# Leaky ReLU in place in PSUM, its remainder on VectorE; one-input query maxima; ScalarE rounds the query exponentials

## The chip, the cores and the metric

The kernel runs on one core of one Trainium2 chip. The metric is the device time of one execution in microseconds (us); lower is better. The engines of the core are TensorE (PE in the profile; its weight loads have a row of their own, PEld), VectorE (DVE), ScalarE (ACT), GpSimd (POOL) and SyncE (SP, which issues the transfers). Each engine works through its own instructions in a fixed order. TensorE, VectorE and ScalarE reach PSUM, where products are accumulated; the operations of GpSimd in this kernel read and write SBUF alone.

## The reference

Two stages follow each other. The first is a linear attention with a feature map; the second is a two-layer network with a leaky ReLU between its products.

```python
def phi(x):                                   # batch 8, heads 8, 576 tokens, 64 wide
    proj = np.einsum('bhsd,df->bhsf', x, w_phi)           # 128 features
    proj = proj - np.max(np.abs(proj), axis=-1, keepdims=True)
    return np.concatenate([np.exp(proj), np.exp(-proj)], axis=-1)
q_p, k_p = (phi(q), phi(k))
kv = np.einsum('bhsf,bhsd->bhfd', k_p, v)
z = np.sum(k_p, axis=2)
num = np.einsum('bhsf,bhfd->bhsd', q_p, kv)
den = np.einsum('bhsf,bhf->bhs', q_p, z)[..., None] + 1e-06
attn = num / den                              # -> x: 4608 tokens x 512
h = x @ w_in                                  # 512 -> 2048
g = np.maximum(0.01 * h, h)
out = g @ w_out                               # 2048 -> 512
```

## The kernel before, in words

**Products in pieces.** Most operands of TensorE are given as a rounded part and a remainder: a value `x` becomes `xh` (a cast to the matmul type fp32r) and `xl = x - xh`, and a product is the sum of `xh*wh`, `xh*wl` and `xl*wh`. The helper `copy_` makes the casts and `tt_` the remainders; all their instructions carry the helper's lines, L67 (ScalarE), L69 (VectorE) and L72 (subtractions and other two-input operations, VectorE or GpSimd), so they are told apart by the names of their tiles. The table `ENG` says which engine takes which key, in turn where several letters stand (`a` ScalarE, `v` VectorE, `p` GpSimd); a copy without an entry goes to ScalarE, a subtraction without one to GpSimd.

**The network.** The 4608 tokens are 18 blocks of 256, and the 2048 hidden features 16 pieces of 128; one step is one piece of one block, 288 steps in all. `layer1` makes 12 products of 256 columns into a PSUM bank `h` (two banks in turn), four each on L615, L616 and L618. ScalarE's Prelu on L622 writes the leaky ReLU to `g` in SBUF, ScalarE casts `gh` from it, and GpSimd takes `gl = g - gh`. `g`, `gh` and `gl` have two buffers each. `layer2` makes 6 products of 512 columns from `gh` and `gl` (L635, L636, L637) into the two `acc` banks of the block, and is called three steps (`LAG`) behind `layer1`. At the end of a block the two banks are copied to `o` and sent out.

**The attention.** It goes by pairs of heads, 32 in all. The first eight pairs have their own forms (`first_k_phase`, `first_q_phase`, `token_q_phase`); the other 24 go through `q_phase`. There the projections of the queries are transposed in blocks of 32x32 by VectorE (L380), a maximum of absolute values is taken in each block row (L382), and six small operations (L384 to L389) bring the maxima of the four groups of 32 partitions together: three copies and two two-input maxima from and to other partitions, then the result is copied back to all 128. L396 subtracts it, L398 transposes back, and ScalarE makes the two exponentials `eq` (L403, L404). `qh` is the cast of `eq`, on VectorE by the table's entry; `ql = eq - qh` is on GpSimd; L415 to L418 multiply them with the sums of the keys. L424 to L427 make the reciprocal, and the quotient goes to the `ring`, from which `split` takes `xh` and `xl` for the network. `k_phase` does the same for keys (L202 to L295) and is advanced together with the queries of the pair before.

**Order.** The kernel is recorded step by step, and a planner then sets the order of each engine's instructions by priorities and its own estimate of durations: attention has a higher priority than the network, so its instructions go first wherever the planner holds them to be ready. The order is fixed when the program is built; on the chip an instruction that waits holds up all that stand behind it on its engine.

Of the kernel before, what the change touches and what calls it, by code (L numbers as in the profile page):

```python
# [9 lines left out]
F32 = mybir.dt.float32  # L10
# [3 lines left out]
AF = mybir.ActivationFunctionType  # L14
ALU = mybir.AluOpType
AX = mybir.AxisListType

P = 128
# [7 lines left out]
T = 256  # L26
# [5 lines left out]
NK = 8  # L32
BUFS = {"kph": 2, "eq": 2, "m4": 2, "g": 2, "gh": 2, "gl": 2, "ql": 2}
PBUFS = {"a": 3, "c": 1, "h": 2, "acc": 2}
ENG = {"vh": "a", "kst": "v", "qh": "v", "o": "av", "kl": "pv", "kpl": "pppv", "ksub": "vvp", "l": "v"}
TINY = 2.0 ** -15
HUGE = 2.0 ** 16 * 1.875
PF = -10 ** 6
# [6 lines left out]
def attention_moe_kernel(ctx: ExitStack, tc: tile.TileContext, q, k, v, vt, w_phi, w_in, w_out, out):  # L45
    nc = tc.nc
# [4 lines left out]
    def ct(shape, dt, name):  # L51
        return cp.tile(shape, dt, tag=name, name=name)

    def st(shape, dt, tag):
        return sp.tile(shape, dt, tag=tag, name=tag, bufs=BUFS.get(tag, 1))
# [3 lines left out]
    def pick(key):  # L59
        n = cnt[key] = cnt.get(key, -1) + 1  # L60
        e = ENG.get(key, "")
        return e[n % len(e)] if e else None

    def copy_(key, o, i):
        e = pick(key) or "a"
        if e == "a":
            nc.scalar.copy(o, i)  # L67
        else:
            (nc.vector if e == "v" else nc.gpsimd).tensor_copy(o, i)  # L69

    def tt_(key, o, a, b, op):
        (nc.vector if pick(key) == "v" else nc.gpsimd).tensor_tensor(o, a, b, op=op)  # L72

    def pt(tag):
        return ps.tile([P, 512], F32, tag=tag, name=tag, bufs=PBUFS[tag])
# [5 lines left out]
    def weight(which, part, ft):  # L81
        g, f = divmod(ft, 4)
        if (which, part, g) not in weights:
            name = f"w{which}{part}{g}"
            weights[which, part, g] = (cp.tile([P, 4, DM], F32R, tag="late", name=name, bufs=4) if g == 3 else
                                       ct([P, 4, DM], F32R, name))
        return weights[which, part, g][:, f]
# [8 lines left out]
    vh = ct([P, 10, 66], F32R, "vh")  # L96
# [44 lines left out]
    for j in range(2):  # L141
        r = slice(64 * j, 64 * j + 64)
        c = slice(F * j, F * j + F)
# [39 lines left out]
    def load_q(i):  # L183
        rq = st([P, S], F32, "rq")
        nc.sync.dma_start(rq, q[i])
        qraw[i] = rq
# [112 lines left out]
    def blocks(x):  # L299
        return x.rearrange("p a b -> p (a b)").rearrange("p (c d) -> p c d", d=32)  # L300
# [60 lines left out]
    def q_phase(i):  # L361
        b, hp = divmod(i, NP)
        rq = qraw.pop(i)
        qs = st([P, 2, S], F32R, "qs")
        for j in range(2):
            o, n = slice(64 * j, 64 * j + 64), slice(64 - 64 * j, 128 - 64 * j)
            copy_("qx", qs[o, j], rq[o])
            nc.vector.tensor_tensor(qs[n, j], rq[o], qs[o, j].bitcast(F32), op=ALU.subtract)  # L368
        if i + 1 < B * NP:
            load_q(i + 1)  # L370
        yield
        tq = st([P, 2, 2, U], F32, "tq")
        m = st([P, 2, 18], F32, "m")
        for j in range(2):
            for u in range(2):
                pq = pt("a")[:, 0:U]
                rs = qs[:, j, U * u : U * u + U]
                nc.tensor.matmul(pq, lhsT=wq_h, rhs=rs, start=True, stop=False)
                nc.tensor.matmul(pq, lhsT=wq_l, rhs=rs, start=False, stop=True)
                nc.vector.transpose(tq[:, j, u], pq)  # L380
                yield
            nc.vector.tensor_reduce(m[:, j], blocks(tq[:, j]), axis=AX.X, op=ALU.max, apply_absolute_value=True)  # L382
        ms = st([64, 2, 18], F32, "ms")
        nc.vector.tensor_copy(ms, m[64:128])  # L384
        nc.vector.tensor_tensor(m[0:64], m[0:64], ms, op=ALU.max)
        nc.vector.tensor_copy(ms[0:32], m[32:64])
        nc.vector.tensor_tensor(m[0:32], m[0:32], ms[0:32], op=ALU.max)
        nc.vector.tensor_copy(m[32:64], m[0:32])
        nc.vector.tensor_copy(m[64:128], m[0:64])  # L389
        yield  # L390
        kvh, kvl = kvs_of[i]
        dn = tq[:, 0]
        qhs = st([P, 2, 2, U], F32R, "qh")
        for j in range(2):
            tj = blocks(tq[:, j])
            nc.vector.tensor_tensor(tj, tj, m[:, j].unsqueeze(2).broadcast_to([P, 18, 32]), op=ALU.subtract)  # L396
            mb = st([P, 2, U], F32, "mb")
            nc.vector.transpose(mb.rearrange("p a b -> p (a b)"), tq[:, j].rearrange("p a b -> p (a b)"))  # L398
            yield
            es = []  # L400
            for u in range(2):
                eq = st([P, 2, U], F32, "eq")
                nc.scalar.activation(eq[:, 0], mb[:, u], AF.Exp)  # L403
                nc.scalar.activation(eq[:, 1], mb[:, u], AF.Exp, scale=-1.0)  # L404
                qh = qhs[:, u]
                ql = st([P, 2, U], F32R, "ql")
                copy_("qh", qh, eq)
                tt_("ql", ql, eq, qh.bitcast(F32), ALU.subtract)
                es.append((qh, ql))
                yield  # L410
            for u in range(2):
                qh, ql = es[u]
                nm = pt("a")[:, 0:U]
                for t in range(2):
                    nc.tensor.matmul(nm, lhsT=kvh[:, j, t], rhs=qh[:, t], start=t == 0, stop=False)  # L415
                    nc.tensor.matmul(nm, lhsT=kvl[:, j, t], rhs=qh[:, t], start=False, stop=False)
                for t in range(2):
                    nc.tensor.matmul(nm, lhsT=kvh[:, j, t], rhs=ql[:, t], start=False, stop=t == 1)  # L418
                rr = slice(64 * j, 64 * j + 64)
                nc.scalar.copy(ring[rr, b % 2, hp, U * u : U * u + U], nm[0:64])  # L420
                nc.scalar.activation(dn[rr, u], nm[64:128], AF.Copy, bias=1e-6)
                yield
        dt = st([P, 2, U], F32, "mb")
        nc.vector.transpose(dt.rearrange("p a b -> p (a b)"), dn.rearrange("p a b -> p (a b)"))  # L424
        rc = st([P, 18], F32, "rc")
        nc.vector.reciprocal(rc, blocks(dt)[:, :, 0])
        nc.vector.transpose(blocks(dt), rc.unsqueeze(2).broadcast_to([P, 18, 32]))  # L427
        x = ring[:, b % 2, hp]
        tt_("x", x, x, dt.rearrange("p a b -> p (a b)"), ALU.mult)
        yield  # L430
# [153 lines left out]
    def attention():  # L584
        for i in range(NP, B * NP + 1):
            gens = [k_phase(i)] if i < B * NP else []
            if i > NP:
                gens.append((token_q_phase if i - 1 < NN else q_phase)(i - 1))
            while gens:
                for it in list(gens):  # L590
                    if next(it, end) is end:
                        gens.remove(it)
                    else:
                        yield i - 1
            yield i
# [16 lines left out]
    def layer1(i, ft):  # L612
        ph = pt("h")[:, 0:T]
        for d in range(NP):
            nc.tensor.matmul(ph, lhsT=weight(0, "h", ft)[:, d * P : d * P + P], rhs=xh[:, d], start=d == 0, stop=False)  # L615
            nc.tensor.matmul(ph, lhsT=weight(0, "l", ft)[:, d * P : d * P + P], rhs=xh[:, d], start=False, stop=False)  # L616
        for d in range(NP):
            nc.tensor.matmul(ph, lhsT=weight(0, "h", ft)[:, d * P : d * P + P], rhs=xl[:, d], start=False, stop=d == NP - 1)  # L618
        g = st([P, T], F32, "g")
        gh = st([P, T], F32R, "gh")  # L620
        gl = st([P, T], F32R, "gl")
        nc.scalar.activation(g, ph, AF.Prelu, alpha=0.01)  # L622
        copy_("gh", gh, g)
        tt_("gl", gl, g, gh.bitcast(F32), ALU.subtract)
        gs[i, ft] = (gh, gl)

    def layer2(i, ft, half=range(TT)):
# [47 lines left out]
    for n, (i, ft) in enumerate(steps):  # L675
        layer1(i, ft)
        advance(min(room(i + 1), NP * (1 + (i + (ft + 1) / NFT) * T / S) + 2))
        if ft == NFT - 1 and i + 1 < NBLK:
            advance(math.ceil((i + 2) * T / S) * NP)
            split(i + 1)  # L680
        if n >= LAG:
            layer2(*steps[n - LAG])
# [39 lines left out]
```

## Time and profile before

| | us |
|---|---|
| median of 3 runs (lowest, highest) | 1253.36 (1252.39, 1255.06) |
| profiled execution | 1253.03 |
| span of its instructions | 1251.2 |
| PE busy | 1184.7 (95%) |
| DVE busy | 840.5 (67%) |
| ACT busy | 804.3 (64%) |
| POOL busy | 691.0 (55%) |

The profile shows one execution. The shares are means over parts that differ: up to about 300 us the first pairs and the conversion of the weights run, from 300 to about 1060 us attention and network are interleaved, and from about 1080 us on only the network is left. A row of the groups reads: line, engine, operation, written tile, read tiles, shapes, count, then busy time in us and the mean of one in ns, then the idle time before these instructions and what ended it. A matmul's row has its whole length, though the next starts earlier, so short stalls of TensorE do not show as idle time in it.

### The profile page before, as it was taken

Reading aid. Unit: us, or ns where it says so; the run is one execution under the profiler, and the core shown is the slowest. Engines: PE = TensorE matmul, PEld = TensorE weight load, DVE = VectorE, ACT = ScalarE, POOL = GpSimd, SP = SyncE. Lnnn points to the kernel's source line nnn. Section 1 sums busy time; section 2 is a strip of 40 time slices with the busy share of each in tenths; the row PEclk is TensorE's granted clock in tenths of the full one; section 3 lists DMA queues with packets and bytes.
Section 4 is the critical chain, followed back from the end, with each engine's and each line's share of the span. In section 5 each row is a group of like instructions: output and inputs, shape, how many; then the busy total and the mean of one; then the engine's idle time right before and its main releaser. Section 6 shows DMA issues by size and latency. Waiting matters only on the chain. (4 is left out here: it accounts for less than half of the span.)

```text
span 1251.2 us, 21516 instructions
## 1 busy us (share of the span) xinstructions
PE 1184.7 (95%) x7654; PEld 1045.7 (84%) x7654; DVE 840.5 (67%) x1349; ACT 804.3 (64%) x2048; POOL 691.0 (55%) x724
## 2 busy tenths in 40 slices
PE   6889899999998999899999999999999999999998
PEld 5577688898887888788898888899997889999997
DVE  7999843478788877788888788854888887300000
ACT  6897865767667776666776667764776767433232
POOL 3233232457685776666676677764676867433232
PEclk9999999999998999999999999999999999999999
DMA  6544510211111101111111111020111110000000
GB/s 189 155 125 140 141 52 13 57 31 30 47 31 47 29 29 31 30 39 29 48 30 48 31 39 39 10 58 28 30 24 37 28 38 1 18 17 1 18 17 18
DMA packets 62779, 57.02 MB, mean 46 GB/s; under 512 B 45136, under 2 KB 46288, under 8 KB 62672
## 3 DMA queue, kind: packets, MB, share of 16 engines
q1 hardware_dynamic: 62672, 55.65, 15.8%
q8 instruction: 60, 0.98, 0.3%
q14 instruction: 47, 0.39, 0.1%
HBM read 46.20 MB, written 9.44 MB: 44 GB/s over the span
## 5 line engine op out<-in xcount | busy, mean ns | idle before, releaser
L72 POOL TENSOR_TENSOR gl<-g,gh 128x256 fp32r<-128x256 f32 x288 | 242.4, 846 | 275.1 <-ACT gh L67 214.7
L615 PE MATMUL h<-xh,w0h 128*128 128x256 f32 x1152 | 295.2, 284 | 6.7 <-ACT dn L567 2.2
L616 PE MATMUL h<-xh,w0l 128*128 128x256 f32 x1152 | 293.5, 282 | 1.3 <-DVE w0l L72 1.3
L615 PEld LDWEIGHTS h<-xh,w0h 128*128 128x128 f32 x1152 | 217.9, 189 | 18.7 <-ACT dn L567 3.0
L635 PE MATMUL acc<-w1h,gh 128*128 128x512 f32 x576 | 229.5, 399 | 2.9 <-DVE o L69 1.8
L636 PE MATMUL acc<-w1l,gh 128*128 128x512 f32 x576 | 228.0, 396 | 0.0
L616 PEld LDWEIGHTS h<-xh,w0l 128*128 128x128 f32 x1152 | 218.0, 189 | 11.5 <-DVE w0l L72 2.1
L637 PE MATMUL acc<-w1h,gl 128*128 128x512 f32 x576 | 218.3, 396 | 0.2 <-POOL gl L72 0.2
L618 PE MATMUL h<-xl,w0h 128*128 128x256 f32 x1152 | 201.7, 283 | 0.7 <-POOL xl L72 0.7
L622 ACT ACTIVATE g<-h 128x256 f32<-128x256 f32 x288 | 108.1, 383 | 133.0 <-PE h L618 93.1
L72 POOL TENSOR_TENSOR ql<-eq,qh 128x576 fp32r<-128x576 f32 x96 | 153.0, 1601 | 71.8 <-DVE qh L69 59.8
L618 PEld LDWEIGHTS h<-xl,w0h 128*128 128x128 f32 x1152 | 164.7, 189 | 3.1 <-POOL xl L72 2.0
L67 ACT CAST gh<-g 128x256 fp32r<-128x256 f32 x288 | 114.8, 404 | 70.4 <-PE acc L636 68.5
L72 POOL TENSOR_TENSOR kpl<-ek,kph 128x512 fp32r<-128x512 f32 x72 | 104.3, 1449 | 34.6 <-ACT kph L67 17.3
L635 PEld LDWEIGHTS acc<-w1h,gh 128*128 128x128 f32 x576 | 108.8, 189 | 16.7 <-DVE o L69 2.7
L637 PEld LDWEIGHTS acc<-w1h,gl 128*128 128x128 f32 x576 | 105.7, 188 | 19.1 <-POOL gl L72 1.3
L636 PEld LDWEIGHTS acc<-w1l,gh 128*128 128x128 f32 x576 | 109.1, 189 | 12.8
L69 DVE CAST qh<-eq 128x576 fp32r<-128x576 f32 x96 | 95.6, 1002 | 35.7 <-ACT eq L404 24.7
L250 ACT ACTIVATE ek<-pmk 128x256 f32<-128x256 f32 (+1 forms) x128 | 53.4, 417 | 64.8 <-POOL kpl L72 27.5
L69 DVE COPY o<-acc 128x512 f32<-128x512 f32 x17 | 11.5, 677 | 124.2 <-DMA out_dram<-o 124.0
L403 ACT ACTIVATE eq<-mb 128x288 f32<-128x288 f32 x96 | 42.2, 439 | 81.6 <-DVE mb L398 77.9
L72 POOL TENSOR_TENSOR ring<-ring,mb 128x576 f32<-128x576 f32 (+2 forms) x45 | 52.1, 1158 | 66.7 <-DVE mb L573 18.3
(227 smaller groups left out, 2505.6 us busy)
## 6 DMA issues: line engine op xcount, KB each, us to landing
out_dram<-o SPq DMA_DIRECT2D x35, 256.0 KB, 2.0
rk<-in_k_dram SPq DMA_DIRECT2D x30, 288.0 KB, 2.8
ring<-in_w_in_dram SPq DMA_DIRECT2D x16, 512.0 KB, 3.6
qh<-in_w_out_dram SPq DMA_DIRECT2D x16, 512.0 KB, 3.6
rq<-in_q_dram SPq DMA_DIRECT2D x28, 288.0 KB, 2.9
rv<-in_v_dram SPq DMA_DIRECT2D x30, 256.0 KB, 3.5
rv<-in_vt_dram SPq DMA_DIRECT2D x60, 32.0 KB, 2.9
f<-in_k_dram SPq DMA_DIRECT2D x2, 288.0 KB, 4.2
```

Source lines behind the costliest of these rows:

```text
L67: nc.scalar.copy(o, i)
L69: (nc.vector if e == "v" else nc.gpsimd).tensor_copy(o, i)
L72: (nc.vector if pick(key) == "v" else nc.gpsimd).tensor_tensor(o, a, b, op=op)
L250: nc.scalar.activation(ek[r, :, 0:F], pmk[r, 2 * s : 2 * s + 2], AF.Exp)
L403: nc.scalar.activation(eq[:, 0], mb[:, u], AF.Exp)
L615: nc.tensor.matmul(ph, lhsT=weight(0, "h", ft)[:, d * P : d * P + P], rhs=xh[:, d], start=d == 0, stop=False)
L616: nc.tensor.matmul(ph, lhsT=weight(0, "l", ft)[:, d * P : d * P + P], rhs=xh[:, d], start=False, stop=False)
L618: nc.tensor.matmul(ph, lhsT=weight(0, "h", ft)[:, d * P : d * P + P], rhs=xl[:, d], start=False, stop=d == NP - 1)
L622: nc.scalar.activation(g, ph, AF.Prelu, alpha=0.01)
L635: nc.tensor.matmul(a, lhsT=gh[:, ts], rhs=weight(1, "h", ft), start=ft == 0, stop=False)
L636: nc.tensor.matmul(a, lhsT=gh[:, ts], rhs=weight(1, "l", ft), start=False, stop=False)
L637: nc.tensor.matmul(a, lhsT=gl[:, ts], rhs=weight(1, "h", ft), start=False, stop=ft == NFT - 1)
```

## The change

The leaky ReLU is written back to its own PSUM bank `h`. ScalarE casts `gh` from there, and the remainder `gl = h - gh` is an operation of VectorE on the bank and `gh`; the tile `g` is gone. The query maxima are brought together by reductions: a copy is a maximum over one element, and a maximum of two is a reduction over two values that lie side by side in one tile, for which `m` and `ms` get a second half. The table gives `qh` to ScalarE.

```diff
-ENG = {"vh": "a", "kst": "v", "qh": "v", "o": "av", "kl": "pv", "kpl": "pppv", "ksub": "vvp", "l": "v"}
+ENG = {"vh": "a", "kst": "v", "qh": "a", "o": "av", "kl": "pv", "kpl": "pppv", "ksub": "vvp", "l": "v"}
 ...
-        m = st([P, 2, 18], F32, "m")
+        mm = st([P, 2, 2, 18], F32, "m")
+        m = mm[:, 0]
 ...
-        ms = st([64, 2, 18], F32, "ms")
-        nc.vector.tensor_copy(ms, m[64:128])
-        nc.vector.tensor_tensor(m[0:64], m[0:64], ms, op=ALU.max)
-        nc.vector.tensor_copy(ms[0:32], m[32:64])
-        nc.vector.tensor_tensor(m[0:32], m[0:32], ms[0:32], op=ALU.max)
-        nc.vector.tensor_copy(m[32:64], m[0:32])
-        nc.vector.tensor_copy(m[64:128], m[0:64])
+        def one(o, x):
+            nc.vector.tensor_reduce(o, x.unsqueeze(3), axis=AX.X, op=ALU.max)
+
+        ms = st([64, 2, 2, 18], F32, "ms")
+        one(mm[0:64, 1], m[64:128])
+        nc.vector.tensor_reduce(ms[0:64, 0], mm[0:64].rearrange("p s j c -> p j c s"), axis=AX.X, op=ALU.max)
+        one(ms[0:32, 1], ms[32:64, 0])
+        nc.vector.tensor_reduce(m[0:32], ms[0:32].rearrange("p s j c -> p j c s"), axis=AX.X, op=ALU.max)
+        one(m[32:64], m[0:32])
+        one(m[64:128], m[0:64])
 ...
-        g = st([P, T], F32, "g")
         gh = st([P, T], F32R, "gh")
         gl = st([P, T], F32R, "gl")
-        nc.scalar.activation(g, ph, AF.Prelu, alpha=0.01)
-        copy_("gh", gh, g)
-        tt_("gl", gl, g, gh.bitcast(F32), ALU.subtract)
+        nc.scalar.activation(ph, ph, AF.Prelu, alpha=0.01)
+        copy_("gh", gh, ph)
+        nc.vector.tensor_tensor(gl, ph, gh.bitcast(F32), op=ALU.subtract)
```

The planner orders all engines anew. In the changed kernel the lines stand up to five further down (L618 becomes L622, L637 becomes L640, the Prelu is L625, and `gl` is L627). Two places are spoken of below. The first is VectorE in `q_phase`, in the interleaved part, from the maxima to the next transposition (`tq` the transposed projections, `m` and `ms` the maxima, `mb` what the exponentials read; `kvl` and `qs` belong to other work). Before:

```order
L385 TENSOR_TENSOR m<-m,ms 64x36
L368 TENSOR_TENSOR qs<-rq,qs 64x576
L386 COPY ms<-m 32x36
L387 TENSOR_TENSOR m<-m,ms 32x36
L388 COPY m<-m 32x36
L294 TENSOR_TENSOR kvl<-c,kvh 128x4x64
L295 TENSOR_TENSOR kvl<-c,kvh 128x4x64
L389 COPY m<-m 64x36
L396 TENSOR_TENSOR tq<-tq,m 128x576 x2
L398 STREAM_TRANSPOSE mb<-tq 128x576
L69 CAST qh<-eq 128x576 x2
L398 STREAM_TRANSPOSE mb<-tq 128x576
```

And of the change:

```order
L385 TENSOR_REDUCE m<-m 64x36
L294 TENSOR_TENSOR kvl<-c,kvh 128x4x64
L295 TENSOR_TENSOR kvl<-c,kvh 128x4x64
L389 TENSOR_REDUCE ms<-m 64x36
L385 TENSOR_REDUCE ms<-ms 32x36
L627 TENSOR_TENSOR gl<-h,gh 128x256
L391 TENSOR_REDUCE m<-ms 32x36
L385 TENSOR_REDUCE m<-m 32x36
L385 TENSOR_REDUCE m<-m 64x36
L400 TENSOR_TENSOR tq<-tq,m 128x576 x2
L402 STREAM_TRANSPOSE mb<-tq 128x576
L627 TENSOR_TENSOR gl<-h,gh 128x256
```

The two casts `qh` between the transpositions are gone, and remainders `gl` now stand among the steps of the query, where VectorE had none.

The second place is TensorE at the start of block 16 (step 256), near the end, where only the network is left. Before, `h_14122` and `h_14147` are the first two steps of the block, and products of the old block (`gh_14078`, `gh_14103` and their remainders) follow:

```order
L618 MATMUL h_14122<-xl_71,w0h0_716 128x256
L618 MATMUL h_14147<-xl_71,w0h0_716 128x256 x2
L635 MATMUL acc_13806<-w1h3_1005,gh_14078 128x512
L636 MATMUL acc_13806<-w1l3_1006,gh_14078 128x512
L637 MATMUL acc_13806<-w1h3_1005,gl_14079 128x512
L635 MATMUL acc_13807<-w1h3_1005,gh_14078 128x512
L636 MATMUL acc_13807<-w1l3_1006,gh_14078 128x512
L637 MATMUL acc_13807<-w1h3_1005,gl_14079 128x512
L635 MATMUL acc_13806<-w1h3_1005,gh_14103 128x512
L636 MATMUL acc_13806<-w1l3_1006,gh_14103 128x512
```

In the change the same steps are `h_13866` and `h_13890`, and `gh_13879` is the cast of `h_13866`:

```order
L640 MATMUL acc_13562<-w1h3_1005,gl_13848 128x512
L622 MATMUL h_13866<-xl_71,w0h0_716 128x256
L622 MATMUL h_13890<-xl_71,w0h0_716 128x256
L640 MATMUL acc_13563<-w1h3_1005,gl_13848 128x512
L638 MATMUL acc_13962<-w1h0_729,gh_13879 128x512
L639 MATMUL acc_13962<-w1l0_730,gh_13879 128x512
L619 MATMUL h_13914<-xh_70,w0h0_716 128x256
L620 MATMUL h_13914<-xh_70,w0l0_717 128x256
```

ScalarE's rows for these two steps in the change:

```order
L625 ACTIVATE h_13866<-h_13866 128x256
L625 ACTIVATE h_13890<-h_13890 128x256
L67 CAST gh_13879<-h_13866 128x256
L67 CAST gh_13903<-h_13890 128x256
```

Before, all the products of two older steps stand between the first two steps of the block and the third; in the change a product that needs the cast `gh_13879` stands two rows behind the last product of `h_13866`, and the third step `h_13914`, which takes the bank of `h_13866`, two rows further.

## Prediction

> **What bounds the kernel now.** I read the busy time by stretches first. Columns: stretch, its length, then busy us of each engine.
>
> ```profile
> core 0: us, PE busy (x) PEld busy (x) DVE busy (x) ACT busy (x) POOL busy (x), PEclk, DMA share, GB/s
> 0.00:300.00 300.00, 272.62 (x1668) 229.01 (x1669) 220.16 (x400) 217.61 (x516) 108.31 (x136) 0.98 0.34 96
> 300.00:1060.00 760.00, 725.23 (x4803) 648.13 (x4802) 604.48 (x921) 522.97 (x1366) 517.13 (x501) 1.00 0.12 33
> 1100.00:1200.00 100.00, 100.00 (x637) 90.42 (x636) 1.38 (x2) 32.83 (x89) 34.80 (x53) 1.00 0.03 11
> ```
>
> At the end (1100 to 1200 us) TensorE never stops, VectorE is free, and nothing but fewer products would help. From 300 to 1060 us TensorE idles 760 - 725.23 = 34.8 us, with VectorE busy 80% of the time, ScalarE 69%, GpSimd 68%. A matmul's row is longer than its turn, which the chain of waits shows: in the last part four products of 256 columns take 0.48 us, 0.12 each, and one of 512 columns 0.24, while the row of L615 further down has a mean of 284 ns for 256 columns. So the idle time of PE leaves out most of a short stall.
>
> ```profile
> 1102.77 0.48 PE h L618 x4
> 1103.24 0.24 PE acc L635
> 1105.59 0.48 PE h L618 x4
> ```
>
> (These also give a step without attention: 1105.59 - 1102.77 = 2.82 us.) The weight loads are shorter than their turn, so their waits show more. The list of waits of PEld from 300 to 1060 us has 27 rows, sum 63.4 us (engine, tile and line that waited, what ended it, us in total, times, longest); the first ten and the last:
>
> ```profile
> PEld c L212 <- issue: 6.7, 9, 2.0
> PEld c L212 <- POOL kpl L72: 5.6, 8, 2.1
> PEld a L378 <- DVE tq L380: 5.2, 6, 1.3
> PEld a L415 <- ACT tq L421: 5.1, 7, 1.3
> PEld a L415 <- DVE pmk L237: 4.9, 9, 0.8
> PEld a L415 <- DVE qh L69: 4.8, 9, 0.9
> PEld a L418 <- POOL ql L72: 4.7, 9, 1.0
> PEld c L212 <- ACT kph L67: 4.0, 9, 1.1
> PEld acc L635 <- DVE o L69: 2.7, 3, 1.5
> PEld a L232 <- ACT tq L421: 2.5, 5, 0.8
> ...
> PEld a L232 <- issue: 0.2, 1, 0.2
> ```
>
> Summed by releaser: VectorE 23.0, GpSimd 13.6, ScalarE 17.9, the rest 8.9. TensorE is the bound, and loses about 63 us in this part to attention results that come later than its fixed order has them, mostly from VectorE and GpSimd.
>
> **Why these two are late.** Durations of VectorE's operations from the views by tile (count, then minimum/median/maximum ns):
>
> ```profile
> L69 DVE CAST qh<-eq x96: 441/990/1700, 275.1 to 1073.2; 128x576 fp32r<-128x576 f32 x96
> L202 DVE TENSOR_TENSOR ks<-rk,ks x48: 752/1717/1967, 213.4 to 1019.5; 64x576 fp32r<-64x576 f32 x48
> L386 DVE COPY ms<-m x24: 170/328/1312, 269.3 to 1063.3; 32x36 f32<-32x36 f32 x24
> L382 DVE TENSOR_REDUCE m<-tq x48: 705/753/755, 261.7 to 1062.0; 128x18 f32<-128x576 f32 x48
> ```
>
> Copies and two-input operations between SBUF tiles are stretched by up to 1.0 to 1.3 us for the same work, about one GpSimd operation (its groups below take 0.85 to 1.6 us); the reduction never is (705 to 755). So while GpSimd works, some forms of VectorE stand still.
>
> **The change, part by part.** The groups that carry its prices (mean ns after the busy time):
>
> ```profile
> L72 POOL TENSOR_TENSOR gl<-g,gh 128x256 fp32r<-128x256 f32 x288 | 242.4, 846 | 275.1 <-ACT gh L67 214.7 <-issue 16.0 <-PE acc L637 11.9
> L72 POOL TENSOR_TENSOR ql<-eq,qh 128x576 fp32r<-128x576 f32 x96 | 153.0, 1601 | 71.8 <-DVE qh L69 59.8 <-PE acc L636 9.9 <-PE a L418 1.3
> L615 PE MATMUL h<-xh,w0h 128*128 128x256 f32 x1152 | 295.2, 284 | 6.7 <-ACT dn L567 2.2 <-ACT w0h L67 2.0 <-ACT xh L67 1.7
> L67 ACT CAST gh<-g 128x256 fp32r<-128x256 f32 x288 | 114.8, 404 | 70.4 <-PE acc L636 68.5
> L622 ACT ACTIVATE g<-h 128x256 f32<-128x256 f32 x288 | 108.1, 383 | 133.0 <-PE h L618 93.1 <-POOL gl L72 36.2 <-PE a L232 1.5
> L69 DVE CAST qh<-eq 128x576 fp32r<-128x576 f32 x96 | 95.6, 1002 | 35.7 <-ACT eq L404 24.7 <-POOL ql L72 4.4 <-POOL gl L72 3.8
> L237 DVE TENSOR_TENSOR pmk<-a,pmk 128x256 f32<-128x256 f32 x96 | 37.1, 406 | 7.5 <-ACT pmk L67 6.5
> L240 DVE TENSOR_REDUCE m<-pmk 128x4 f32<-128x512 f32 x48 | 32.7, 681 | 1.3
> L240 DVE TENSOR_REDUCE m<-pmk 64x2 f32<-64x256 f32 x24 | 10.0, 417 | 0.8
> L67 ACT CAST qs<-rq 64x576 fp32r<-64x576 f32 x48 | 32.3, 673 | 4.1 <-PE a L379 3.4
> L67 ACT COPY pmk<-a 128x256 f32<-128x256 f32 x96 | 32.6, 373 | 3.4 <-PE a L232 2.8
> ```
>
> And how much of it lies between 300 and 1060 us (`gl` with its PE, PEld and POOL columns; `qh` with DVE's; the four maxima steps L384 to L387 with DVE's):
>
> ```profile
> 300.00:1060.00 760.00, 135.22 (x355) 65.15 (x355) 157.17 (x178) 1.00 0.12 33
> 300.00:1060.00 760.00, 87.78 (x88) 1.00 0.12 33
> 300.00:1060.00 760.00, 39.59 (x88) 1.00 0.12 33
> ```
>
> *The remainder.* GpSimd loses 178 operations, 157.2 us, in this part. VectorE gains 178; the nearest row is L237, also a PSUM bank and an SBUF tile at 128x256, 0.406 us: 72.3 us.
>
> *The cast `qh`.* VectorE loses 87.8 us. ScalarE gains 88 casts; a 576-wide cast there takes 0.673: 59.2 us.
>
> *The maxima.* L384 to L387 cost 39.59/22 = 1.80 us a query pair; L388 and L389, whose undisturbed length is that of the other copies, I count at 0.3 each, so 2.4 in all. Reductions: 512 elements take 681 and 256 take 417 ns, 1.03 ns each over a fixed 153; 36 elements (four instructions) give 0.19 and 72 (two) 0.23, together 1.2 us. Saved: 1.2 x 22 = 26 us. The result is on the path from the last transposition to the exponentials, so each pair also gets its exponentials 1.2 us sooner.
>
> *Prelu into PSUM, and `gh` from it.* No row shows ScalarE writing PSUM. From PSUM to SBUF it takes 0.373 to 0.383, from SBUF to SBUF 0.404; I take 0.383 for Prelu, bounds 0.35 and 0.41 (one such difference either way), and 0.373 for `gh`: 178 x 0.03 = 5 us less, between 11 less and 0. The Trainium skill (PSUM — Partial Sum Buffer, Specifications) says that ScalarE writes faster to PSUM than to SBUF; no run here shows it, and by it the lower bound, 11 us less, would hold.
>
> *What stays and is stretched less.* L202 loses 1463 - 752 = 0.71 us on each of 48, in the view by groups:
>
> ```profile
> L202 DVE TENSOR_TENSOR ks<-rk,ks 64x576 fp32r<-64x576 f32 x48 | 70.2, 1463 | 18.1 <-ACT ks L67 16.9
> ```
>
> That is 34 us. GpSimd's load in this part falls from 517 to 360 us, by 30%; I take 30% of it, 10 us (0 to 34). The other stretched forms come on top and I leave them in the bounds.
>
> The part from 300 to 1060 us then has VectorE at 604 - 88 - 26 + 72 - 10 = 552 us (73%), GpSimd at 360 (47%), ScalarE at 523 + 59 - 5 = 577 (76%). What is stretched beyond its undisturbed length falls more: `qh` 96 x (1.002 - 0.441) = 54, the maxima 24 x (2.4 - 6 x 0.17) = 33, L202 34; of these 121 us, 24 (70% of L202's) stay.
>
> *Sum on TensorE's path.* The waits that VectorE and GpSimd end are 36.6 us. They can fall by as little as VectorE's busy time does (9%, 3 us) or by as much as the stretching (80%, 29 us). They are lateness against a fixed order, which stretching makes, so I take 60%: **-22.0**. ScalarE's 17.9 us grow with its busy time (577/523): **+1.8**.
>
> *Block starts.* The changed order of TensorE, shown above, gives the price of the held bank. Between the last product of `h_13866` and the first that needs its cast lie one product of 256 and one of 512 columns, 0.12 + 0.24 = 0.36 us. The cast needs the rest of the last product (0.28 - 0.12 = 0.16), Prelu 0.38, the Prelu of the next step, which ScalarE has in front (0.38), and the cast 0.37: 1.29 us. Stall: 0.93 us. Before, six products of 512 columns (1.4 us) for each of two steps lie there, no stall. Behind it `gl` (0.41) has 0.47 us of products as cover: nothing. For three block starts after attention's end: **+2.8**. In the fourteen earlier ones other products can lie between, so 0 to 13 us; I take **+2**. Within a block of the last part a bank is wanted again after 2.82 x 2 - 1.41 = 4.2 us, and Prelu, cast and `gl` take 1.2: nothing.
>
> *Before 300 us* the planner lays down some of the 288 steps while VectorE also converts weights; there `gl` comes in front of conversions that TensorE will need, and takes stretching away. I take **+2**, bounds -6 and +6 (15 remainders of 0.41 us, either as cost or as what GpSimd no longer blocks).
>
> The profiled execution took 1253.03 us, 0.33 under the median of the runs. 1253.0 - 22.0 + 1.8 + 2.8 + 2 + 2 = 1239.6: **1240 us**, its own range 1229 to 1250.
>
> **Rivals.**
>
> *The whole lateness goes.* ScalarE's waits are themselves mostly for VectorE and GpSimd, so all 54.5 us would fall by 70%: -38, and +7 as above: 1222 us. For it: the longest wait of ScalarE here is for VectorE's L398, which stands right behind the maxima. Against it: ScalarE's own load rises.
>
> ```profile
> ACT eq L403 <- DVE mb L398: 73.2, 39, 5.1
> ```
>
> *ScalarE becomes the late one.* At 76% it is the busiest engine beside TensorE; `ql` waits for its casts instead of VectorE's. If its 17.9 us double and the block starts cost 5, the 22 are used up: 1254 us. Against it: its operations hardly vary in length, so the planner knows them well.
>
> *The held bank, slower.* `gl` waits for ScalarE's `gh`, now at the head of VectorE's queue, and behind it stand the transpositions and maxima of attention. On GpSimd this wait was long and free:
>
> ```profile
> POOL gl L72 <- ACT gh L67: 214.7, 99, 6.3
> DVE pmk L237 <- ACT pmk L67: 31.9, 19, 4.1
> ```
>
> VectorE's L237 waits for a copy of ScalarE in the same way, 31.9 us over 120 of them (the 96 above and 24 with 64 rows), 0.27 us each. At that price 178 remainders make VectorE stand 48 us, nearly all of the 52 us by which its busy time falls; attention would be no earlier, and TensorE would find `h` taken. With no gain, 36% of the 48 us on TensorE's path (VectorE's share, 23.0 of 63.4), and 5 at block starts: 1253 + 17 + 5 = 1275 us; where half of the remainders wait so, 1253 + 9 + 5 = 1267. It decides once `gl` ends more than 4.2 us behind its step. The Trainium skill (VectorE: DVE Perf Modes, Rules for kernel authors) speaks for this side: copy from PSUM to SBUF first where several operations follow. By it the bank, now read and written by three operations in a row, is the dear place. Against it: the planner puts `gl` where it holds it to be ready.
>
> **How the numbers follow.** Forecast 0.48, all lateness 0.22, ScalarE 0.13, held bank 0.17. A measurement of this kernel tells about 0.2% (2.5 us) from no change. ScalarE's case spreads over both sides: 0.03 faster, 0.09 the same, 0.01 slower. Faster: 0.48 + 0.22 + 0.03 = 0.73; same 0.09; slower 0.18. The range goes from a little below the second case to the beginning of the slower one: 1217 to 1259.
>
> **What would show it.** Right: PEld's waits for VectorE and GpSimd from 300 to 1060 us near 15 us; `qh` on ScalarE near 0.67; the six reductions at 0.19 to 0.23 with no long ones; `gl` on VectorE at 0.41; L202's mean near 1.25; a stall of 0.9 us before the first L638 of each of the last three blocks. Wrong: waits of L619 or L638 for `gl` or `gh` spread over the whole interleaved part (held bank), or PEld's waits for ScalarE near 40 us (ScalarE).

## The result

The changed kernel takes 1210.99 us (median of 4 runs, 1209.61 to 1212.16), the kernel before beside it 1252.88: a ratio of 0.966, 95% interval 0.9645 to 0.968. That is 42 us faster, where the prediction had 13 and a range whose lower end was 1217. The direction and the place were right, and the forecast gain was a third of what came. The experiments then showed that a good part of the 42 us is not the change's own: the order in which the kernel before happened to be laid out was a slow one.

### The profile page after: what moved, and what is told of

Read it like the earlier page. It is cut to its first block, busy times and chain, and to the rows that moved or that the text cites. A ratio compares the mean times of both kernels' runs of the same rounds, so it can differ in the third digit from the quotient of the medians.

```text
span 1207.8 us, 21459 instructions
## 1 busy us (share of the span) xinstructions
PE 1160.7 (96%) x7654; PEld 1041.8 (86%) x7654; DVE 785.4 (65%) x1541; ACT 850.7 (70%) x2144; POOL 437.9 (36%) x436
## 4 chain that ended last, share of the span: by engine, by line
PE 76%; DVE 11%; ACT 7%; issue 3%; DMA 2%; POOL 0%; DVEq 0%; ACTq 0%
PE h L619 10%; PE h L620 10%; PE h L622 10%; PE acc L638 9%; PE acc L640 9%; PE acc L639 9%; PE c L212 6%; PE a L232 2%; PE a L422 2%; PE a L419 2%; PE a L420 2%; PE a L333 1%; DVE ql L165 1%; PE a L379 1%; PE a L380 1%
## 5 line engine op out<-in xcount | busy, mean ns | idle before, releaser
L619 PE MATMUL h<-xh,w0h 128*128 128x256 f32 x1152 | 292.3, 284 | 6.8 <-DVE gl L627 4.5
L627 DVE TENSOR_TENSOR gl<-h,gh 128x256 fp32r<-128x256 f32 x288 | 118.5, 416 | 237.4 <-ACT gh L67 210.9
L638 PE MATMUL acc<-w1h,gh 128*128 128x512 f32 x576 | 230.3, 400 | 6.8 <-ACT gh L67 6.1
L619 PEld LDWEIGHTS h<-xh,w0h 128*128 128x128 f32 x1152 | 217.9, 189 | 17.3 <-DVE gl L627 7.7
L625 ACT ACTIVATE h<-h 128x256 f32<-128x256 f32 x288 | 105.3, 368 | 157.2 <-PE h L622 155.3
L640 PE MATMUL acc<-w1h,gl 128*128 128x512 f32 x576 | 204.3, 397 | 0.0
L622 PE MATMUL h<-xl,w0h 128*128 128x256 f32 x1152 | 200.1, 282 | 0.1
L72 POOL TENSOR_TENSOR ql<-eq,qh 128x576 fp32r<-128x576 f32 x96 | 146.1, 1538 | 73.0 <-ACT qh L67 47.8
L622 PEld LDWEIGHTS h<-xl,w0h 128*128 128x128 f32 x1152 | 164.3, 189 | 0.9 <-POOL xl L72 0.3
L72 POOL TENSOR_TENSOR kpl<-ek,kph 128x512 fp32r<-128x512 f32 x72 | 95.4, 1325 | 146.4 <-ACT kph L67 67.5
L638 PEld LDWEIGHTS acc<-w1h,gh 128*128 128x128 f32 x576 | 108.8, 189 | 28.4 <-ACT gh L67 9.8
L67 ACT CAST gh<-h 128x256 fp32r<-128x256 f32 x288 | 105.2, 373 | 25.6 <-PE acc L639 21.3
L72 POOL TENSOR_TENSOR xl<-ring,xh 128x256 fp32r<-128x256 f32 (+3 forms) x96 | 61.2, 669 | 155.0 <-PE h L622 135.3
L72 POOL TENSOR_TENSOR ring<-ring,mb 128x576 f32<-128x576 f32 (+2 forms) x45 | 49.8, 1108 | 175.0 <-DVE mb L342 45.5
L640 PEld LDWEIGHTS acc<-w1h,gl 128*128 128x128 f32 x576 | 99.5, 189 | 8.5 <-issue 0.4
L202 DVE TENSOR_TENSOR ks<-rk,ks 64x576 fp32r<-64x576 f32 x48 | 53.7, 1118 | 36.5 <-ACT ks L67 35.3
L250 ACT ACTIVATE ek<-pmk 128x256 f32<-128x256 f32 (+1 forms) x128 | 53.4, 417 | 24.3 <-POOL kpl L72 10.3
L212 PE MATMUL c<-kph,vh 128*66 128x256 f32 x240 | 62.3, 282 | 4.0 <-DVE kvl L295 2.2
```

Of the source, the lines that this page charges most:

```text
L202: nc.vector.tensor_tensor(ks[n, j], rk[o], ks[o, j].bitcast(F32), op=ALU.subtract)
L212: nc.tensor.matmul(kvp[0 : lt.shape[1], 256 * j : 256 * j + 256], lhsT=lt, rhs=rt, start=first and j == 0, stop=last, skip_group_check=True)
L625: nc.scalar.activation(ph, ph, AF.Prelu, alpha=0.01)
L627: nc.vector.tensor_tensor(gl, ph, gh.bitcast(F32), op=ALU.subtract)
L638: nc.tensor.matmul(a, lhsT=gh[:, ts], rhs=weight(1, "h", ft), start=ft == 0, stop=False)
L640: nc.tensor.matmul(a, lhsT=gl[:, ts], rhs=weight(1, "h", ft), start=False, stop=ft == NFT - 1)
```

## The profile after

Busy time by stretches of the changed kernel, with the columns of the prediction:

```profile
0.00:300.00 300.00, 274.07 (x1688) 231.70 (x1689) 230.47 (x457) 225.79 (x541) 76.74 (x96) 0.98 0.35 97
300.00:1060.00 760.00, 745.93 (x5083) 684.19 (x5082) 531.69 (x1031) 583.27 (x1487) 352.07 (x324) 1.00 0.12 34
1100.00:1200.00 100.00, 97.89 (x624) 88.10 (x623) 15.86 (x37) 28.10 (x78) 5.66 (x8) 1.00 0.03 11
```

From 300 to 1060 us TensorE idles 14.1 us in place of 34.8, VectorE is at 70%, GpSimd at 46%, ScalarE at 77%. At the end TensorE now stops 2.1 us in 100 where it had not stopped at all. The groups that were priced (mean ns behind the busy time):

```profile
L627 DVE TENSOR_TENSOR gl<-h,gh 128x256 fp32r<-128x256 f32 x288 | 118.5, 416 | 237.4 <-ACT gh L67 210.9 <-PE acc L640 20.6 <-PE a L422 3.7
L625 ACT ACTIVATE h<-h 128x256 f32<-128x256 f32 x288 | 105.3, 368 | 157.2 <-PE h L622 155.3
L67 ACT CAST gh<-h 128x256 fp32r<-128x256 f32 x288 | 105.2, 373 | 25.6 <-PE acc L639 21.3 <-PE acc L640 0.5
L67 ACT CAST qh<-eq 128x576 fp32r<-128x576 f32 x96 | 61.9, 667 | 0.8 <-PE a L420 0.5
L202 DVE TENSOR_TENSOR ks<-rk,ks 64x576 fp32r<-64x576 f32 x48 | 53.7, 1118 | 36.5 <-ACT ks L67 35.3
L385 DVE TENSOR_REDUCE m<-m 64x36 f32<-64x36 f32 x48 | 8.8, 184 | 1.3
L391 DVE TENSOR_REDUCE m<-ms 32x36 f32<-32x72 f32 x24 | 5.2, 216 | 0.6
```

The prices of the new operations were met: the remainder on VectorE 0.416 us (0.41), the cast on ScalarE 0.667 (0.673), the reductions 0.18 and 0.22 (0.19 and 0.23). L202 came out at 1.12, below the 1.25 of the prediction. The waits of PEld from 300 to 1060 us, all ten rows:

```profile
PEld h L619 <- DVE gl L627: 6.8, 6, 1.9
PEld acc L638 <- ACT gh L67: 3.9, 6, 1.2
PEld c L212 <- ACT kph L67: 3.6, 2, 2.6
PEld c L212 <- ACT o L67: 1.5, 1, 1.5
PEld a L419 <- ACT qh L67: 1.2, 1, 1.2
PEld a L379 <- DVE pmk L237: 1.1, 1, 1.1
PEld acc L638 <- DVE o L69: 0.9, 1, 0.9
PEld c L212 <- DVE kph L270: 0.7, 1, 0.7
PEld c L212 <- DVE kpl L72: 0.6, 1, 0.6
PEld h L622 <- POOL xl L72: 0.3, 1, 0.3
```

Their sum is 20.6 us against 63.4: a difference of 42.8, as much as the whole gain. (Before 300 us the same list falls from 45.4 to 42.3 us, and behind 1060 us it rises from 0.4 to 4.4.) The list has turned over: attention (L212, L378, L415, L418) was most of it, and now the first two rows are the network's own, the bank `h` held for `gl` and the cast `gh`. They are few (6 times each), not spread over the 178 steps.

The new stall at the block starts, in the timeline of the changed kernel (start, us, engine, line, operation; idle time before it and its releaser in brackets):

```profile
1112.93 0.40 PE L622 MATMUL h<-xl,w0h 128*128 128x256 f32 x2
1113.13 0.59 ACT L67 COPY o<-acc 128x512 f32<-128x512 f32 x1 [4.78 <-PE acc L640]
1113.17 0.39 PE L640 MATMUL acc<-w1h,gl 128*128 128x512 f32 x1
1113.62 0.65 ACT L625 ACTIVATE h<-h 128x256 f32<-128x256 f32 x2
1114.18 0.65 ACT L67 CAST gh<-h 128x256 fp32r<-128x256 f32 x2
1114.62 0.50 PE L638 MATMUL acc<-w1h,gh 128*128 128x512 f32 x1 [1.05 <-ACT gh L67]
```

TensorE idles 1.05 us before the block's first L638, and three such stalls in the last part make 3.0 us. The prediction had 0.93 from the order alone, with two Prelus and a cast; an output copy of 0.59 us stands in front of them too.

## The experiments

Three theories were put down: stretching (S: VectorE's copies and two-input operations stand still behind GpSimd, and that makes attention late), load (L: what counts is how much work VectorE has), and chain (C: what counts is the way from `h` to `gl`).

### Each part alone

The remainder alone:

```diff
-        nc.scalar.activation(g, ph, AF.Prelu, alpha=0.01)
-        copy_("gh", gh, g)
-        tt_("gl", gl, g, gh.bitcast(F32), ALU.subtract)
+        nc.scalar.activation(ph, ph, AF.Prelu, alpha=0.01)
+        copy_("gh", gh, ph)
+        nc.vector.tensor_tensor(gl, ph, gh.bitcast(F32), op=ALU.subtract)
```

> The kernel before with the leaky ReLU in PSUM and its remainder on VectorE alone; cast of the exponentials and maxima as before. Theory S (stretching: VectorE's copies and two-input SBUF operations stand still behind GpSimd operations, and that is what makes attention late): GpSimd's busy time between 300 and 1060 us falls from 517 to about 360 us, the means of qh (1002 ns) and L202 (1463 ns) fall by about 30% of their excess, to some 830 and 1250 ns; about 1238 us. Theory L (load: what counts is how much work VectorE has): 178 more operations of 0.41 us there, busy time up to some 640 of 760 us; 1253 to 1265 us. Theory C (chain: what counts is that h no longer waits for GpSimd by way of g): most of the 42 us, about 1215.

The maxima alone (the six operations of the change's diff) and the cast alone (`"qh": "a"`):

> The kernel before with the one-input maxima alone. Theory S: the six operations fall from 2.4 to 1.2 us a pair, with no long ones; the exponentials of each pair come 1.2 us sooner: 1240 to 1246 us. Theory L: 26 us less of 604 us on VectorE: about 1250. Theory C: 1253.

> The kernel before with the cast of the exponentials on ScalarE alone. Theory S: 88 us leave VectorE, 54 of them stretching; ql starts about 0.4 us earlier after each exponential: 1235 to 1242 us. Theory L: 88 of 604 us leave VectorE, about 1240, the largest of the three parts. Theory C: 1253.

Measured: 1223.5 us (0.976, interval 0.9745 to 0.9774), 1219.9 (0.9732, 0.9716 to 0.9748) and 1227.5 (0.9795, 0.9779 to 0.981). Each part brings 26 to 34 us, together they bring 42. No theory has the three times: S forecast too little for each part, by 8 to 20 us, L has no gain for the remainder, and C none for the maxima and the cast.

### Each part taken out of the change

> The changed kernel with g, its cast and the remainder on GpSimd as before; the cast on ScalarE and the one-input maxima stay. Theory S: most forms that stretched are gone, the GpSimd load is not, L202 stays near 1.4 us: about 1225 us. Theory L: VectorE has 72 us less than in the changed kernel: 1211 or below. Theory C: near 1245.

> The changed kernel with the maxima as before (copies and two-input maxima). Theory S: the six operations take about 2 us a pair at the lower GpSimd load; 1216 to 1222 us. Theory L: VectorE has 15 to 20 us more of 532: about 1213. Theory C: 1211.

> The changed kernel with the cast of the exponentials on VectorE. Theory S: the casts are stretched less than before, mean about 0.8 us, VectorE gets some 70 us and ScalarE loses 59: 1220 to 1230 us. Theory L: VectorE at 532 + 70 of 760, as busy as before: near 1250. Theory C: 1211.

Measured: 1218.1 us (0.9719, 0.9704 to 0.9733) without the remainder, 1227.0 (0.979, 0.9774 to 0.9807) without the maxima, 1219.2 (0.9729, 0.9713 to 0.9745) without the cast. Theory L falls: with the cast back on VectorE it is busy 623 of 760 us, more than the 604 of before, and the kernel is 34 us faster. Theory C falls with 1218 for a kernel that has the old chain (it had 1245). Theory S had the kernel without the maxima 5 us too fast and the one without the remainder 7 us too slow. But any edit whatever seemed to bring 25 to 35 us.

### GpSimd loaded again, and a form that does not stretch

The changed kernel with an idle operation on GpSimd:

```diff
         nc.vector.tensor_tensor(gl, ph, gh.bitcast(F32), op=ALU.subtract)
+        load = st([P, T], F32, "g")
+        nc.gpsimd.tensor_tensor(load, gh.bitcast(F32), gh.bitcast(F32), op=ALU.subtract)
```

> The changed kernel with one more GpSimd operation a step, a subtraction of 128x256 that reads the cast gh twice and writes a tile that nothing reads; it adds work and leaves none out. GpSimd's busy time between 300 and 1060 us goes back from 352 to about 500 us. Theory S: L202's mean goes from 1.12 back to about 1.45 us, that of L72 pmk and the others up too, 20 to 25 us more on VectorE, of which about half ends on TensorE's path: 1218 to 1226 us. Theory L (VectorE's own work is the same) and theory C: 1211, within 3 us.

Measured: 1218.6 us (0.9718, 0.9704 to 0.9733). Its stretch and its L202:

```profile
300.00:1060.00 760.00, 743.36 (x5036) 679.98 (x5035) 543.93 (x1029) 585.23 (x1488) 483.00 (x517) 0.99 0.12 34
L202 DVE TENSOR_TENSOR ks<-rk,ks 64x576 fp32r<-64x576 f32 x48 | 60.1, 1251 | 52.9 <-ACT ks L67 52.1
```

GpSimd is back at 483 us, L202 at 1.25 us (not 1.45), and 7.6 us are lost, inside what S expected. The operation also holds `gh` until GpSimd has read it, and it stands in GpSimd's own queue; but in this trace only GpSimd's `ql` and `kpl` wait for it, 1.2 and 0.5 us in all. The clock granted to TensorE is lower too, 0.985 to 0.990 of full speed in the four executions against 0.992 to 0.993 in the changed kernel; 0.0045 of 1215 us is 5.5 us at most (an estimate), so this pair alone does not settle it.

The kernel before with the cast as a reduction over one element:

```diff
-                copy_("qh", qh, eq)
+                nc.vector.tensor_reduce(qh, eq.unsqueeze(3), axis=AX.X, op=ALU.max)
```

> The kernel before with the cast of the exponentials still on VectorE, but as a reduction over one element, a form that the trace never shows stretched (576 elements: 0.70 to 0.755 us). Theory S: mean 0.75 in place of 1.00 us though the undisturbed cast takes 0.44: VectorE has 22 us less, and GpSimd is blocked less: 1242 to 1249 us. Theory L by undisturbed lengths: 29 us more work on VectorE: 1257 to 1265.

Measured: 1224.5 us (0.9771, 0.9747 to 0.9794), the cast at 0.748 us as expected, and the time 18 us below what S gave. By then the gains were too alike to be the work of such different edits.

### The order alone

The first two kernels leave the work of before as it is but for the order. In one, the two output copies of a block exchange engines (`"o": "va"`); in the other a small memset on VectorE precedes the maxima. The third is the change with the same exchange. A fourth theory is put against S here: order (O: the planner happened to give the kernel before a slow order, and a new one takes most of its lateness away).

> The kernel before with the two letters of the entry for the output copies exchanged (av to va), so that the two copies of a block change engines: the same work on each engine to one copy, but the planner lays the program out anew. Theory S (stretching, whatever the order): 1253, within 5 us. Theory O (the order that the planner gave the kernel before is an unlucky one, and any edit that makes it plan anew gets rid of most of its lateness): 1220 to 1235 us.

> The kernel before with one small VectorE operation more a query pair (a memset of 64x36 in a tile that nothing reads), in front of the maxima: 24 operations of some 0.1 to 0.2 us. Theory S: 1253 to 1256 us. Theory O: 1220 to 1235 us.

> The changed kernel with the same exchange of the letters for the output copies. Theory S: 1211, within 5 us. Theory O: between 1211 and 1225, as orders of one and the same work scatter; were it 1230 or more, the change itself would have brought little.

Measured: 1235.6 us (0.9859, 0.9844 to 0.9874), 1253.0 (0.9996, 0.9987 to 1.0005), and 1211.2 (0.9667, 0.9651 to 0.9683). The memset left the waits and the durations what they were in the kernel before (the cast's mean 1001 ns there, 1002 before), so its order is as good as unchanged, and so is its time. The exchange of two letters brought 18 us, to just above the range of theory O; the memset, which also makes the planner plan anew, brought nothing, so not any edit does it. To see how far this goes, the letters of `kpl` were turned round, from `pppv` to `vppp` and `ppvp`, in both kernels: the same count on each engine, another chunk on VectorE.

> The kernel before with the letters for kpl turned round by one (pppv to vppp): VectorE takes the first of four remainders in place of the fourth; the same count on each engine, another order. Theory S (stretching): 1253, within 10 us. Theory O (the order of the kernel before is an outlier): 1215 to 1235 us.

> The same with the third of four (ppvp). Theory S: 1253, within 10 us. Theory O: 1215 to 1235 us. A scatter of the orders without the change that goes down to 1220 would leave the single parts (1220 to 1228) unexplained by their own work.

> The changed kernel with the letters for kpl turned round by one (vppp), to be held against the same turn of the kernel before (1229.5). If the change is worth 10 to 25 us whatever the order: 1208 to 1218. If it only got rid of an unlucky order: 1222 to 1232.

> The changed kernel with the third of four (ppvp), to be held against the same turn of the kernel before (1225.1). If the change is worth 10 to 25 us whatever the order: 1204 to 1215. If it only got rid of an unlucky order: 1218 to 1228.

| letters | without the change, us | with it, us | difference | PEld's waits 300 to 1060 us, without, with |
|---|---|---|---|---|
| as given | 1252.9 | 1211.0 | -42 | 63.4, 20.6 |
| `o` exchanged | 1235.6 | 1211.2 | -24 | 38.3, 19.1 |
| `kpl` turned, vppp | 1229.5 | 1213.5 | -16 | 36.7, 24.1 |
| `kpl` turned, ppvp | 1225.1 | 1209.4 | -16 | 29.5, 22.1 |

(Ratios to the kernel before: 0.9813, interval 0.9795 to 0.983, and 0.977, 0.9755 to 0.9786, for the two turns without the change; 0.9688, 0.9672 to 0.9704, and 0.9655, 0.964 to 0.9669, with it.) The change wins in all four pairs. Without it, orders of the same work scatter over 28 us, with it over 4. Of the 42 us, 16 to 24 are what the change is worth in the other three orders; the remaining 18 to 26 come with leaving one slow order, which turned or exchanged letters do too (18 to 28 us). The granted clock is a small rival to this: its mean is 0.988 to 0.989 in the three orders without the change and 0.990 to 0.993 with it. A difference of 0.003 of 1225 us is 4 us at most (an estimate), far less than 16.

What made that order slow is not the stretching. In the kernel with `ppvp`, without the change, the busy times and VectorE's durations are near those of the kernel before:

```profile
300.00:1060.00 760.00, 740.53 (x4982) 676.81 (x4981) 600.38 (x942) 537.46 (x1397) 525.21 (x514) 0.99 0.12 34
L69 DVE CAST qh<-eq x96: 433/844/1761, 273.7 to 1044.8; 128x576 fp32r<-128x576 f32 x96
L202 DVE TENSOR_TENSOR ks<-rk,ks x48: 751/1348/2050, 212.6 to 992.9; 64x576 fp32r<-64x576 f32 x48
PEld a L232 <- DVE ks L202: 5.0, 4, 1.6
PEld a L415 <- DVE qh L69: 2.9, 5, 1.0
PEld a L415 <- ACT tq L421: 2.9, 1, 2.9
```

VectorE 600 us (604), GpSimd 525 (517), casts up to 1.76 us, and still TensorE waits half as long. The forms that stretch (the casts `qh`, L202, `pmk` on L72 and the six maxima steps) take 267 us together, 272 before. Nor does the vector part of a pair go faster: from the end of a pair's last transposition L380 to the end of its last `ql`, mean of the 24 pairs, it takes 20.1 us before, 20.3 with `ppvp`, and 19.2 in the changed kernel. What differs, then, should be what TensorE has in front of the products that wait; this is argued and not shown. Which of the placements in the order of the kernel before costs the 18 to 28 us was not found, and stays open.

### The two probes again in another order

Because a single pair tells so little, the loaded GpSimd and the reduction were repeated with the exchanged letters.

> The changed kernel with the idle GpSimd subtraction a step and the letters of the output copies exchanged, to be held against the exchange alone (1211.2). Theory S: 1216 to 1222. Theory O: 1208 to 1216, no sign.

> The kernel before with the cast of the exponentials as a reduction on VectorE and the letters of the output copies exchanged, to be held against the exchange alone (1235.6). Theory S: below that by 8 to 15 us, 1220 to 1228. Theory O: 1225 to 1245, no sign.

Measured: 1219.2 us against 1211.2 of the exchange alone (+8.0, after +7.6 in the first pair), and 1241.3 against 1235.6 (+5.7, after -28 in the first pair). The load on GpSimd costs the changed kernel 8 us in both orders, more than the 4 us of scatter there, and in the second pair the granted clock is the same (0.990 in the mean of both). That the stretching is how it costs is not shown: VectorE's busy time from 300 to 1060 us grows by 12 us in the first pair (531.7 to 543.9) and by 2.4 in the second (535.7 to 538.1), for the same loss. The reduction in place of the cast, for which S had 1220 to 1228, has no sign of its own; the 28 us of its first run were the order's. So the times of the single parts alone (1220 to 1228) cannot be read as their worth either: orders without any part reach 1225.

### More buffers

The changed kernel with `"gh": 3, "gl": 3`:

> The changed kernel with three buffers each for gh and gl in place of two (the room of the tile g that is gone). If the cast gh waits for its buffer and the bank h is held for it, the stalls before L638 and L619 (5.6 us for gl, 3.9 us for gh on the weight loads from 300 to 1060 us, and the block starts of the last part) go: 1203 to 1208 us. If they come from ScalarE's and VectorE's queues, 1211 within 3 us. Theory O: anything from 1205 to 1220.

Measured: 1213.9 us (0.9683, 0.9667 to 0.9699). The three waits of L638 at the last block starts are still there, 3.2 us on PE in place of 3.0. They come from ScalarE's queue (copy, two Prelus, cast), not from buffers. In the interleaved part the two rows that the buffers were meant for did shrink, from 10.7 to 3.9 us, though `gh` now ends a wait of other products:

```profile
PEld c L212 <- ACT gh L67: 4.0, 2, 2.9
PEld acc L638 <- ACT gh L67: 2.3, 4, 1.1
PEld h L619 <- DVE gl L627: 1.6, 2, 1.4
```

The list's sum is 18.7 us against 20.6, and yet the kernel is 2.9 us slower. Its granted clock is lower, 0.984 to 0.986 in all four executions against 0.992 to 0.993; 0.0075 of 1212 us is 9 us at most (an estimate). So what the buffers are worth at an equal clock stays open. No kernel beat the changed one clearly; with `ppvp` it ran at 1209.4, 1208.3 to 1211.1.

## Why the prediction was wrong in size

**What held.** That TensorE is the bound and loses some 63 us to late attention between 300 and 1060 us; that the change takes work and stretching off VectorE and load off GpSimd there (forecast 552, 360 and 577 us of VectorE, GpSimd and ScalarE; 532, 352 and 583 came); that the held bank stays without weight inside a block of the last part; and the stall at the last block starts (+2.8; 3.0 us came). Prelu into PSUM took 368 ns against 383 before; the Trainium skill (PSUM — Partial Sum Buffer, Specifications (TRN2)) has ScalarE faster to PSUM, the trace agrees, with half of the gain that the lower bound allowed.

**The step that failed is the sum on TensorE's path.** It put the waits that VectorE and GpSimd end (36.6 us) at 60% less, -22, let ScalarE's 17.9 us grow by 1.8, and had no term for the 8.9 us of the rest. The first fell to 10.4, -26.2; ScalarE's fell to 10.2, -7.7, though ScalarE got busier; the rest vanished, -8.9. Behind the step stood the premise that these waits are lateness against a fixed order "which stretching makes", so that they shrink with the work and the stretching. The four pairs of orders show that the size of the waits is not set by these. PEld's waits from 300 to 1060 us by releaser, without the change and with it (the rest are rows that name TensorE itself or, as "issue", no engine):

| letters | VectorE and GpSimd, us | ScalarE, us | the rest, us |
|---|---|---|---|
| as given | 36.6, 10.4 | 17.9, 10.2 | 8.9, 0 |
| `o` exchanged | 26.2, 8.5 | 5.1, 10.6 | 7.0, 0 |
| `kpl` turned, vppp | 16.9, 13.7 | 10.3, 8.8 | 9.5, 1.6 |
| `kpl` turned, ppvp | 13.2, 10.8 | 9.5, 10.7 | 6.8, 0.6 |

With the old work in another order, the waits that VectorE and GpSimd end are 13.2 to 26.2 us and ScalarE's 5.1 to 10.3. So both amounts from which the step started belong in good part to one order, and the fall of ScalarE's waits, which the forecast missed by 9.5 us, comes with leaving that order: in the other three pairs they change by +5.5, -1.5 and +1.2. The rest, which had no term, falls by 6 to 9 us in all four.

The rival that saw ScalarE waiting for VectorE has a part in this, but here too the order alone does much. Of the 73.2 us for which `eq` waited for `mb`, this is left in the changed kernel and in the kernel with `ppvp` without the change:

```profile
ACT eq L407 <- DVE mb L402: 19.7, 15, 2.9
ACT eq L403 <- DVE mb L398: 46.2, 36, 3.2
```

**What the step left out.** It took the 63 us as the cost of the work. They were the cost of one order of it: the same work in three other orders waits 30 to 38 us. That the forecast of 13 us lies near the 16 to 24 us of these orders is luck: with their own waits the step's shares would give about 8, 2 and 0 us (an estimate), where 24, 16 and 16 came. In these three pairs the listed waits fall by 19.2, 12.6 and 7.4 us, less than the times; how the change brings its 16 to 24 us is shown only in part and stays open. The front of this document says that the planner orders all engines anew, and the prediction priced only the two places that it looked at. In a kernel like this the new order is a term of the sum, with a width of some 28 us here and, for an order as slow as this one, a sign.

**The other terms.** Before 300 us the prediction had +2; PEld's waits there fell by 3.1 us (and by 3.7 to 5.0 in the other pairs), so the change gains a little, inside the bounds of -6 and +6. For the held bank in the interleaved part it had +2 (0 to 13); the rows of L619 and L638 for `gl` and `gh` come to 10.7 us, and of the 6.8 of L619, by a count of the steps, 4.7 lie behind the first three steps of a block. The rival with all lateness gone (1222) came nearest by its number; ScalarE as the late one is refuted by its 10.2 us. The held bank (1267 to 1275) is refuted by the 10.7 us, which stand in a dozen waits, and the three operations on the bank are no dearer than those that they replace (0.368, 0.373 and 0.416 us; 0.383, 0.404 and 0.846 before). Its premise did come true: from 300 to 1060 us VectorE stood still before `gl`, for longer than the 48 us that the rival had.

```profile
DVE gl L627 <- ACT gh L67: 77.1, 53, 3.6
```

What did not follow is that attention, and TensorE with it, would pay for this standing still.

## What to carry to other kernels

Where a planner lays out the whole program, measure two or three neutral relayouts (two letters turned, no work changed) on both sides before a gain of a few per cent is given to an edit; here it cut 42 us to 16 to 24. Read the loss of a saturated TensorE from the waits of its weight loads: over the table their sum falls from 63.4 to some 20 us as the time falls, though it does not tell the four changed kernels apart and accounts for only half of the gain with `ppvp`. Follow a releaser back before its share is left out. The four orders of the changed kernel lie close together (1209 to 1214 us); that this comes from the forms that its VectorE operations now have is not shown.

## What the runs showed of the hardware

The one-input reductions that move 36 elements to other partitions took 178 to 184 ns in the mean, 188 at the longest, where copies and two-input maxima of the same size went up to 1.3 us. The remainder from a PSUM bank took 377 to 427 ns in all 288 cases, and 379 to 427 where GpSimd was loaded to 483 us. The Trainium skill (SBUF — State Buffer, Who interferes with whom) says that a VectorE instruction with at most one SBUF input, outside its two-port modes, does not contend with GpSimd, and one with two SBUF inputs contends with a GpSimd instruction that reads SBUF: the trace agrees, with L202 (two SBUF inputs) at 752 to 1967 ns. What was not expected is how little this alone decided: a kernel with the long operations still in it, in another order, was 28 us faster.
